# Retention attention with expert routing on one core: the second batch's heads swapped in q and k, state products and tails on quadrants of the array

## The chip, the cores and the metric

The kernel runs on one core of a Trainium2 chip. The metric is device time in microseconds of one execution. Three runs of the kernel before took 655.72, 658.25 and 662.20 us; the median is 658.25.

## What is computed

A retention layer (causal attention without softmax, its scores weighted by powers of a factor of each head) over 8 batches, 8 heads, 576 positions and 64 dimensions, and behind it a routed layer of 8 experts, each with a capacity of 576 of the 4608 tokens.

```python
scores = scale * np.matmul(q, k.transpose(0, 1, 3, 2))
gamma = 1.0 - 2.0 ** (-5.0 - np.arange(H, dtype=np.float32))
rel = pos[:, None] - pos[None, :]
Dmat = np.where(rel >= 0, gamma[:, None, None] ** rel[None, :, :], 0.0)
ret = scores * Dmat[None, :, :, :]
x = np.matmul(ret, v)                       # [tokens, heads * dims] afterwards
logits = x @ w_gate                         # each token goes to one expert with room, best logit first
h = np.maximum(x[mask] @ w1[e], 0.0)
out[mask] = h @ w2[e]
```

## The kernel before

The attention part works on 16 units. A unit `u` is one pair of batches and one pair of heads (`hp = u % 4`); four units make one pair of batches, `bp`. A unit has nine blocks of 128 columns: block `2*c + b` holds positions `128*c` to `128*c + 127` of batch `b` (`c` from 0 to 3), and block 8, the tail, the last 64 positions of both batches. Both heads of the pair stand on the partitions: head `h` of q and k on partitions `64*h` to `64*h + 63`.

The retention is computed in chunks of 128 positions. Each block gets scores within the block and, from a running state of the earlier chunks, what reaches across:

- `A` (L576): scores, k times q, 64 rows by 128 columns of the array. Head 0 uses rows 0 to 63, head 1 rows 64 to 127, and each writes its own PSUM tile `pA`. Four blocks fill the two tiles; the tail has its own (`pA0t`, `pA1t`). VectorE multiplies each by a mask with the powers of gamma of that head (L581, `am`).
- `ST` (L593): state products, v times scaled k, 128 rows by 64 columns, summed in PSUM over the chunks. Two ScalarE copies (L599), one for each head, scale the state into the two diagonal blocks of a 128x128 tile `S` whose other blocks are zero.
- `XS` (L620, L617 for the tail): state times q, 128 rows by 64 columns, because the zero blocks keep the heads apart. It writes the PSUM tile `pX`, three blocks to a tile, two tiles at a time.
- `XW` (L630): v times `am`, added into the same tile. `scale` (L642) then takes three blocks at a time out of PSUM into `xT`, times a factor for each position.
- `kscale2` (L556): GpSimd scales k into a new tile `ks`, a half unit ahead.

All these are fp32; each matmul of the program stands as two rows in the trace. The main loop runs over 16 units in two halves: blocks 0 to 3 and blocks 4 to 8. The scores are a half ahead: in the first half of a unit `A` does blocks 4 to 8 of that unit, in the second blocks 0 to 3 of the next. So a unit begins where the scores of its second half begin. In a half come, in this order: loads, the tail's XS of the unit before (first half), A, XS, ST, XW, ST, and then the side work that a table `fill` puts at this place. The order within each engine is that of the program.

The side work is for the pair of batches that was finished before: logits (L659 matmuls, L665, L672 transposes, L674), transposes of x on VectorE that are written to DRAM through SP's queue (L683, L688), and counts for the routing: `count_first` (L202 to L223) finds each token's best logit and its expert for three chunks of tokens at a time, `count_first_pe` (L234, L236) adds them up on TensorE.

Loads of q, k, v and of k by positions (`n`) of unit `u + 2` are put into SP's queue in unit `u`; q, k and v have three buffers each, `n` two. Constants (`cst`) have, for each pair of heads, two masks for the blocks, three factors and two masks for the tail, 896 columns in all. They are loaded between the first units.

## Time and profile before

| what | us |
|---|---|
| median of three runs (lowest, highest) | 658.25 (655.72, 662.20) |
| profiled execution | 662.15 |
| its span, first to last instruction | 660.4 |
| mean granted TensorE clock | 0.987 of full speed |
| TensorE matmuls busy | 622.7 (94% of the span) |
| VectorE busy | 420.4 (64%) |
| ScalarE busy | 272.6 (41%) |
| GpSimd busy | 174.9 (26%) |

The profile is of one execution. A row of a timeline gives the start of the first of some instructions that follow each other, how long they lasted together, the engine, the line of the kernel, the operation, the tile written and those read, and the shape; in brackets stand the idle time of the engine before it and what ended that. Matmuls overlap, and their ends are modelled; what counts is when the next one starts.

### The profile page before, as it was taken

To read this page: it belongs to the slowest core of one execution; us is meant where nothing else is said; L and a number is where in the kernel's file an instruction comes from. 1 tells how busy PE (TensorE), PEld (TensorE's weight loads), DVE (VectorE), ACT (ScalarE), POOL (GpSimd) and SP (SyncE) were. 2 spreads that over 40 slices of the span, in tenths; PEclk is the share of its full clock that TensorE was granted. 3 is DMA by queue.
4 is the path that set the end of the run, shared out by engine and by line. 5 is a ranking of instruction groups with operands and counts; after the bars stand their busy time and mean duration, and the time that the engine had idled before them with its cause. 6 is when DMAs were issued, how large, how long until landed. Compare 5 with 4: busy or idle time off the path is not lost.

```text
span 660.4 us, 14578 instructions
## 1 busy us (share of the span) xinstructions
PE 622.7 (94%) x5624; PEld 533.1 (81%) x5628; DVE 420.4 (64%) x1594; ACT 272.6 (41%) x488; POOL 174.9 (26%) x225
## 2 busy tenths in 40 slices
PE   7999898988888998999999999998999999999995
PEld 5887877776568876987998798788879989978984
DVE  3577979788775986887897798687774302311300
ACT  2333242423245344553455157225624734653501
POOL 2321222120031135134143142232224134231111
PEclk8999899999997999999999999999999999999998
DMA  9996999964369359689499568928865995893521
GB/s 335 402 403 176 317 295 283 351 195 129 129 193 224 71 190 251 165 235 241 130 235 225 165 163 204 256 82 204 198 196 128 217 261 149 187 254 122 97 64 40
DMA packets 51703, 134.75 MB, mean 204 GB/s; under 512 B 5810, under 2 KB 19762, under 8 KB 51634
## 3 DMA queue, kind: packets, MB, share of 16 engines
q1 hardware_dynamic: 36530, 81.65, 36.5%
q0 software_dynamic: 14960, 51.91, 35.8%
q8 instruction: 44, 0.72, 0.4%
q10 hardware_dynamic: 144, 0.26, 0.1%
q14 instruction: 25, 0.20, 0.1%
HBM read 81.90 MB, written 18.87 MB: 153 GB/s over the span
## 4 chain that ended last, share of the span: by engine, by line
PE 64%; DVE 14%; issue 9%; DMA 8%; ACT 2%; POOL 2%; SPq 1%; POOLq 0%; DVEq 0%; ACTq 0%
PE py L1021 23%; PE ph L982 22%; PE pX L630 4%; PE pA L576 3%; PE pX L620 3%; DMA cst<-in_cst 2%; PE pS L593 2%; PE r L335 2%; PE pt L953 2%; DVE xr L683 1%; DMA w1l<-raw 1%; PE pT L659 1%; DMA out_y<-yt,idx 1%; DMA kin<-in_qk 1%; DMA w2l<-raw 1%
## 5 line engine op out<-in xcount | busy, mean ns | idle before, releaser
L1021 PE MATMUL py<-w2h,hb 128*128 128x512 f32 x576 | 188.3, 399 | 0.0
L982 PE MATMUL ph<-xh,w1h 128*128 128x320 f32 (+1 forms) x512 | 153.3, 303 | 3.9 <-ACT xh L955 1.6
L982 PE MATMUL ph<-xh,w1l 128*128 128x320 f32 (+1 forms) x512 | 150.8, 298 | 3.2 <-DMA w1l<-raw 3.2
L982 PE MATMUL ph<-xl,w1h 128*128 128x320 f32 (+1 forms) x512 | 150.8, 298 | 0.5 <-issue 0.4
L1021 PE MATMUL py<-w2l,hb 128*128 128x512 f32 (+1 forms) x320 | 125.5, 392 | 0.3 <-DMA w2l<-raw 0.2
L1021 PEld LDWEIGHTS py<-w2h,hb 128*128 128x128 f32 x576 | 104.0, 188 | 20.8
L982 PEld LDWEIGHTS ph<-xh,w1h 128*128 128x128 f32 x512 | 97.4, 192 | 5.3 <-ACT xh L955 2.0
L982 PEld LDWEIGHTS ph<-xh,w1l 128*128 128x128 f32 x512 | 97.5, 192 | 3.4 <-DMA w1l<-raw 3.4
L982 PEld LDWEIGHTS ph<-xl,w1h 128*128 128x128 f32 x512 | 97.5, 192 | 1.8 <-issue 1.2
L986 ACT ACTIVATE hb<-ph 128x256 fp32r<-128x256 f32 (+1 forms) x128 | 51.5, 409 | 110.9 <-PE ph L982 102.3
L989 DVE SCALAR_TENSOR_TENSOR hb<-ph,hb 128x256 fp32r<-128x256 f32 (+1 forms) x192 | 58.7, 351 | 59.5 <-ACT hb L986 54.6
L599 ACT ACTIVATE S<-pS,cst 64x128 f32<-64x128 f32 x128 | 46.4, 362 | 91.4 <-PE pS L593 89.8
L998 POOL DMA_INDIRECT out_y<-yt,idx x40 | 41.1, 1026 | 119.5 <-ACT yt L1038 77.4
L1021 PEld LDWEIGHTS py<-w2l,hb 128*128 128x128 f32 (+1 forms) x320 | 56.7, 177 | 14.1 <-DMA w2l<-raw 1.5
L1038 ACT ACTIVATE yt<-py 128x512 f32<-128x512 f32 x32 | 19.1, 597 | 106.2 <-PE py L1021 79.5
L556 POOL TENSOR_TENSOR ks<-nin,cst 128x512 f32<-128x512 f32 x32 | 33.2, 1057 | 108.9 <-DMA nin<-in_vk 103.0
L926 POOL DMA_DIRECT2D w2l<-raw x32 | 28.8, 900 | 124.5 <-ACT hb L986 115.6
L937 POOL DMA_INDIRECT xg<-xd,idx x40 | 40.5, 1013 | 70.1 <-ACT w1h L921 36.8
L581 DVE TENSOR_TENSOR am<-pA,cst 128x512 f32<-128x512 f32 x64 | 41.0, 682 | 22.5 <-PE pA L576 16.0
L1041 DVE TENSOR_TENSOR yt<-yt,py 64x512 f32<-64x512 f32 x8 | 5.4, 678 | 70.2 <-ACT yt L1040 70.1
L926 POOL DMA_DIRECT2D w1l<-raw x31 | 27.5, 901 | 57.0 <-ACT w1l L925 47.0
L576 PE MATMUL pA<-qin,kin 64*128 64x128 f32 x512 | 39.1, 291 | 1.7 <-DMA qin<-in_qk 1.5
(186 smaller groups left out, 947.5 us busy)
## 6 DMA issues: line engine op xcount, KB each, us to landing
raw<-in_w SPq DMA_DIRECT2D x64, 512.0 KB, 5.9
w2l<-raw POOLq DMA_DIRECT2D x32, 512.0 KB
w1l<-raw POOLq DMA_DIRECT2D x31, 512.0 KB
kin<-in_qk SPq DMA_DIRECT2D x14, 576.0 KB, 7.8
qin<-in_qk SPq DMA_DIRECT2D x14, 576.0 KB
vin<-in_vk SPq DMA_DIRECT2D x14, 576.0 KB, 11.5
nin<-in_vk SPq DMA_DIRECT2D x14, 512.0 KB, 8.1
xd<-xr SPq DMA_DIRECT2D x36, 192.0 KB, 3.9
```

Of the source, the lines that this page charges most:

```text
L556: nc.gpsimd.tensor_tensor(KS[u][:, a:b], LD[u, 'n'].rearrange("p (a d) -> p a d", d=64)[:, a:b], ks[:, u % HP, a:b, None].to_broadcast([12 ...
L576: nc.tensor.matmul(PA[0][h][:, j], LD[u, 'k'][r, s], LD[u, 'q'][r, s], start=True, stop=True, skip_group_check=True)
L581: nc.vector.tensor_tensor(am, PA[0][h], m[:, None, h, :].to_broadcast([128, n, 128]), op=ALU.mult)
L599: nc.scalar.activation(st[64*h:64*h+64, :, 64*h:64*h+64], PS[u][64*h:64*h+64], AF.Copy, scale=ss[64*h:64*h+64, hp, c:c+1])
L630: nc.tensor.matmul(px[64*h:64*h+64, :], v[:, blk*128+64*h:blk*128+64*h+64], AM[g, h], start=False, stop=blk < 8, skip_group_check=True)
L926: nc.gpsimd.dma_start(lo, raw, accum_op=ALU.add)
L937: nc.gpsimd.indirect_dma_start(out=xg[:n, j, :], out_offset=None, in_=xd[:, :], in_offset=bass.IndirectOffsetOnAxis(ap=found[e][:n, j:j+1] ...
L982: T.matmul(ps, w, x, start=(k == 0), stop=(k == 11))
L986: A.activation(hb[:, f, c], ps, AF.Relu)
L989: V.scalar_tensor_tensor(hb[:, f, to+a:to+b], ps[:, a:b], 0.0, hb[:, f, 256*s+a:256*s+b].bitcast(F32), op0=ALU.max, op1=ALU.subtract)
L998: st = nc.gpsimd.indirect_dma_start(out=out[:, :], out_offset=bass.IndirectOffsetOnAxis(ap=found[e][:n, t:t+1], axis=0), in_=y[:n], in_off ...
L1021: T.matmul(ps[:m], a, w, start=(k == 0), stop=(k == last), skip_group_check=True)
```

## The change

q and k of the second batch of a unit have the two heads swapped on the partitions. So with `r` for the half of the rows, head `h` and batch `b`, `r = h ^ b`: the states of the two heads of both batches fill all four quadrants of a 128x128 tile, without zeros, and state times q is four matmuls of 64 rows by 64 columns that use the four quadrants. The powers of gamma move from the masks and from k into v, which GpSimd scales in place, and into a factor for each position; the masks hold ones and zeros and are the same for all heads. One VectorE instruction masks both heads, one ScalarE copy takes a state out. `pA` and `pX` are tiles of two banks each, one of each kind; `pX` holds four blocks of a half and, in the second half, the tail. The tail's products are quadrants too, and come at the end of their own unit behind the eviction of the second half. The counts take nine chunks of tokens at once, except for the last pair of batches. `n` gets a third buffer, and v is fetched ahead of it.

```diff
-    c = np.arange(4)
-    ks = g.reshape(HP, 1, 1, 2)[None] ** (-(128.0 * c[None, None, :, None, None] + p[:, None, None, None, None]))
...
+    vs = g.reshape(HP, 1, 2)[None] ** -at[:, None, :, None].astype(np.float64)
+    m1 = p[:, None] <= p[None, :]
+    m2 = p[:, None] % 64 <= np.arange(64)[None, :]
+    ex = 0.125 * g.reshape(HP, 2)[:, p // 64].T[:, :, None] ** np.arange(S)
...
+    cross = lambda a: np.where(second, a[:, :, ::-1], a)
...
     def count_first(s, c0, c1):
-        s.nc.vector.tensor_tensor(G, s.cand128[:, None, :].to_broadcast([128, 3, 128]),
-                                  s.m[:, c0:c1, None].to_broadcast([128, 3, 128]), op=ALU.is_le)
...
+        for c in range(c0, c1, 3):
+            G = s.pool.tile([128, 3, 128], BF16, name="G0", bufs=3)
...
-        part(80 + 896*hp + (0 if hp else 256), 976 + 896*hp)
+        part(CST + S*hp, CST + S*hp + S)
...
-    fetch("k0 q0 c n0 v0 k1 q1 h0 n1 v1 K0 Q0 h1 N0 V0 K1 Q1 N1 V1")
+    fetch("k0 q0 c v0 n0 k1 q1 h0 v1 n1 K0 Q0 h1 V0 N0 K1 Q1 V1 N1")
...
+    half = lambda x: slice(64*x, 64*x + 64)
+    FOUR = ((0, 0), (1, 0), (1, 1), (0, 1))
+    def vscale(u, a, b):
+        v = LD[u, 'v'][:, 128*a:128*b].rearrange("p (a d) -> p a d", d=64)
+        nc.gpsimd.tensor_tensor(v, v, vs[:, u % HP, 2*a:2*b, None].to_broadcast([128, 2*(b-a), 64]), op=ALU.mult)
...
+    def A(u, hf):
+        pa = two.tile([128, 2, 4, 128], F32, name="pA", tag="A", bufs=1)
...
+        nc.vector.tensor_tensor(AM[u, hf], pa, m1[:, None, None, :].to_broadcast([128, 2, 4, 128]), op=ALU.mult)
+    def A2(u):
...
+                nc.tensor.matmul(pa[half(r), h], k[half(r), s], q[half(r), s], start=True, stop=True, skip_group_check=True)
...
+    def ST(u, c):
...
+                nc.tensor.matmul(PS[u][half(h ^ b), b], n[:, s], v[:, s], start=(c == 0 and b == 0), stop=False, skip_group_check=True)
+        st = P['w'].tile([128, 2, 64], F32, name="S", bufs=4)
+        nc.scalar.activation(st, PS[u], AF.Copy)
...
+    def across(u, cs):
+        for c in cs:
+            for h, b in FOUR:
+                r = half(h ^ b)
+                o, a = (PX[u, c//2][half(h), b, 128*(c % 2):128*(c % 2)+128], 256*c + 128*b) if c < 4 else (PX[u, 1][half(h), b, 256:320], 1024 + 64*b)
+                nc.tensor.matmul(o, SI[u, c-1][r, b, :], q[r, a:a+o.shape[1]], start=c in (1, 2), stop=False, skip_group_check=True)
...
+    def within2(u):
+        for h, b in FOUR:
+            r = half(h ^ b)
+            nc.tensor.matmul(PX[u, 1][half(h), b, 256:320], LD[u, 'v'][r, 1024+64*h:1088+64*h], AM[u, 2][r, h],
+                             start=False, stop=False, skip_group_check=True)
+    def evict(u, c0, c1):
...
+        nc.vector.tensor_tensor(dst, src, e, op=ALU.mult)
...
     for u in range(16):
+        for hf in range(2):
...
+            A(u + hf, 1 - hf)
+            if hf == 0:
+                A2(u)
+            PX[u, hf] = two.tile([128, 2, 512], F32, name="pX", tag="X", bufs=1)
+            across(u, (2, 3) if hf else (1,))
+            ST(u, 1 + 2*hf)
+            within(u, hf)
+            if u == 15 and hf:
+                for c in (2, 3):
+                    evict(u, c, c + 1)
+            else:
+                evict(u, 2*hf, 2*hf + 2)
+            ST(u + hf, 2 - 2*hf)
+            if hf:
+                within2(u)
+                across(u, (4,))
+                evict(u, 4, 5)
+            fills(gs)
```

The new functions stand on these lines of the changed kernel: A L564 and L566, A2 L575 and L577, ST L587, across L599, within L608, within2 L615, evict L628.

On TensorE, at the end of a unit, before: the tail's L630 follows the other blocks, then the state products of the next unit, the tail's XS (which belongs to the next unit's first half) and the next scores.

```order
L630 MATMUL pX<-am0t,vin 64x128
L630 MATMUL pX<-am1t,vin 64x128
L593 MATMUL pS<-vin,ks 64x64 [waits DMAHW1_49,Activation_49,Pool_49]
L593 MATMUL pS<-vin,ks 64x64 x3
L617 MATMUL pX<-qin,S_120 64x64 x4
L576 MATMUL pA_1101<-qin,kin 128x128 [waits DVE_49]
L576 MATMUL pA_1102<-qin,kin 128x128 [waits DVE_49]
```

The same place after:

```order
L608 MATMUL pX<-am,vin 64x128 x8
L587 MATMUL pS<-vin,nin 64x64 [waits DMAHW5_49,DMAHW6_49,Activation_49,Pool_49]
L587 MATMUL pS<-vin,nin 64x64 x3
L615 MATMUL pX<-amt,vin 64x64 [waits DVE_49]
L615 MATMUL pX<-amt,vin 64x64 x3
L599 MATMUL pX<-qin,S 64x64 x4
L564 MATMUL pA<-qin,kin 128x128 [waits PE_49]
L564 MATMUL pA<-qin,kin 128x128 x7
```

The tail's L615 has moved behind the state products, and it waits for VectorE.

On VectorE, in the middle of a unit of the second pair of batches, with side work between two evictions, before (`xr` are the transposes, `mx` to `G` a count of three chunks, `om` to `FT` the routing's digits and tables):

```order
L683 STREAM_TRANSPOSE xr<-xT 128x4x4x32
L223 TENSOR_TENSOR G_1013<-rc_f,m 128x384 [waits DVE_49]
L214 TENSOR_TENSOR oh<-t_498,mx_499 128x24 [waits DVE_49]
L156 TENSOR_SCALAR om<-m 128x9
L158 TENSOR_TENSOR om<-m,om 128x9 [waits DVE_49]
L177 TENSOR_TENSOR dg<-om,sm 128x5x9 [waits DVE_49]
L177 TENSOR_TENSOR dg<-dg,sm 128x5x9 [waits DVE_49]
L179 TENSOR_TENSOR DF<-dg,inc 128x5x9 [waits DVE_49]
L181 TENSOR_TENSOR D_512<-dg,inc 128x3x18
L193 TENSOR_TENSOR FT_519<-kt,DF 128x512 [waits DVE_49]
L642 TENSOR_TENSOR xT<-pX,cst 128x384 [waits PE_49]
L581 TENSOR_TENSOR am_1111<-pA_1101,cst 128x512 [waits PE_49]
```

After, in the second half of such a unit, the count of nine chunks between two evictions:

```order
L197 TENSOR_REDUCE m<-Lg 128x9 [waits DVE_49]
L199 TENSOR_TENSOR t_473<-Lg,m 128x72 [waits DVE_49]
L201 TENSOR_TENSOR t_473<-t_473,decb 128x72 [waits DVE_49]
L205 TENSOR_SCALAR m<-m 128x9
L207 TENSOR_REDUCE mx_474<-t_473 128x9 [waits DVE_49]
L665 STREAM_TRANSPOSE xr<-xT 128x4x4x32
L219 TENSOR_TENSOR G_941<-rc_f,m 128x384 [waits DVE_49]
L209 TENSOR_TENSOR oh<-t_473,mx_474 128x72 [waits DVE_49]
L219 TENSOR_TENSOR G_944<-rc_f,m 128x384
L566 TENSOR_TENSOR am<-pA,cst 128x1024 [waits PE_49]
L628 TENSOR_TENSOR xT<-pX,cst 128x2x2x128 [waits PE_49]
L628 TENSOR_TENSOR xT<-pX,cst 128x128 [waits PE_49]
```

The seven small instructions of a count stand once, for 9 and 72 columns instead of 3 and 24, and two evictions follow the am.

## Rows read from the trace of the kernel before

**Rows 1.** The table by stages, each row a stretch of the span in us, its length, and then the busy time (and instructions) of TensorE's matmuls, its weight loads, VectorE, ScalarE and GpSimd; last the granted clock, the DMA share and GB/s. The second and the third are attention, without and with side work; the fourth ends it.

```profile
9.00:42.00 33.00, 31.82 (x549) 28.59 (x546) 20.27 (x65) 11.62 (x34) 9.39 (x10) 0.96 1.03 404
42.00:146.00 104.00, 98.44 (x1632) 82.56 (x1630) 85.61 (x228) 36.64 (x98) 22.95 (x22) 0.98 0.87 282
146.00:158.00 12.00, 9.59 (x145) 6.20 (x141) 9.92 (x35) 3.15 (x8) 0.00 (x0) 1.00 0.43 100
```

**Rows 2.** The timeline of unit 3, from the scores of its second half at 34.10 to those of unit 4 at 41.67: TensorE's matmuls, and of ScalarE and VectorE what the text uses. Behind it the row at which unit 15 begins, and the group of all state copies (count, busy us, mean ns).

```profile
34.10 1.16 PE L576 MATMUL pA<-qin,kin 64*128 64x128 f32 x16
...
35.09 0.27 PE L576 MATMUL pA0t<-qin,kin 64*128 64x128 f32 x1
...
35.21 0.27 PE L576 MATMUL pA0t<-qin,kin 64*128 64x128 f32 x1
...
35.41 0.66 PE L620 MATMUL pX<-qin,S 128*64 128x128 f32 x8
...
35.90 0.40 PE L593 MATMUL pS<-vin,ks 128*64 128x64 f32 x8
36.13 1.05 PE L630 MATMUL pX<-am,vin 128*64 128x128 f32 x16
36.41 0.75 ACT L599 ACTIVATE S<-pS,cst 64x128 f32<-64x128 f32 x2 [1.63 <-PE pS L593]
...
37.30 0.45 PE L593 MATMUL pS<-vin,ks 128*64 128x64 f32 x8
...
37.69 1.16 PE L576 MATMUL pA<-qin,kin 64*128 64x128 f32 x16
...
38.78 1.09 PE L620 MATMUL pX<-qin,S 128*64 128x128 f32 x16
38.88 1.29 DVE L581 TENSOR_TENSOR am<-pA,cst 128x512 f32<-128x512 f32 x2 [0.57 <-PE pA L576]
...
39.70 0.40 PE L593 MATMUL pS<-vin,ks 128*64 128x64 f32 x8
39.93 1.05 PE L630 MATMUL pX<-am,vin 128*64 128x128 f32 x16
...
40.59 0.56 DVE L642 TENSOR_TENSOR xT<-pX,cst 128x384 f32<-128x384 f32 x1 [0.42 <-PE pX L630]
...
41.06 0.45 PE L593 MATMUL pS<-vin,ks 128*64 128x64 f32 x8
...
41.31 0.43 PE L617 MATMUL pX<-qin,S 128*64 128x64 f32 x8
...
41.67 1.16 PE L576 MATMUL pA<-qin,kin 64*128 64x128 f32 x16
...
145.22 0.38 PE L576 MATMUL pA<-qin,kin 64*128 64x128 f32 x2
...
L599 ACT ACTIVATE S<-pS,cst 64x128 f32<-64x128 f32 x128 | 46.4, 362 | 91.4 <-PE pS L593 89.8
```

**Rows 3.** VectorE's groups by form between 42 and 146 us: line, operation, tiles, shape and count; behind the bar the busy us, the mean ns of one, and the idle time before them.

```profile
L581 DVE TENSOR_TENSOR am<-pA,cst 128x512 f32<-128x512 f32 x44 | 28.2, 680 | 6.7 <-PE pA L576 6.5
L642 DVE TENSOR_TENSOR xT<-pX,cst 128x384 f32<-128x384 f32 x33 | 18.1, 547 | 3.1 <-PE pX L630 2.9
...
L214 DVE TENSOR_TENSOR oh<-t,mx 128x24 bf16<-128x24 bf16 x9 | 3.2, 360 | 0.0
L581 DVE TENSOR_TENSOR am0t<-pA0t,cst 128x128 f32<-128x128 f32 x11 | 3.1, 278 | 0.0
...
L206 DVE TENSOR_TENSOR t<-t,decb 128x24 bf16<-128x24 bf16 x9 | 2.7, 297 | 0.0
L210 DVE TENSOR_SCALAR m<-m 128x3 f32<-128x3 f32 x9 | 2.3, 257 | 0.0
...
L204 DVE TENSOR_TENSOR t<-Lg,m 128x24 bf16<-128x24 f32 x9 | 1.8, 203 | 0.3
...
L212 DVE TENSOR_REDUCE mx<-t 128x3 bf16<-128x24 bf16 x9 | 1.6, 175 | 0.0
L202 DVE TENSOR_REDUCE m<-Lg 128x3 f32<-128x24 f32 x9 | 1.3, 144 | 0.0
L236 DVE TENSOR_TENSOR room<-room,cnt 128x8 f32<-128x8 f32 x8 | 1.2, 148 | 3.0 <-PE cnt L234 3.0
```

**Rows 4.** The timeline around the longest wait of XS, at 72.74, and the row of a table by stretches (as in rows 1) from 72 to 76 us.

```profile
70.14 0.51 DVE L223 TENSOR_TENSOR G<-rc_f,m 128x384 bf16<-128x384 f32 x1
...
72.14 0.55 DVE L642 TENSOR_TENSOR xT<-pX,cst 128x384 f32<-128x384 f32 x1
...
72.74 0.44 PE L620 MATMUL pX<-qin,S 128*64 128x128 f32 x4 [1.90 <-DVE xT L642]
...
72.00:76.00 4.00, 3.26 (x41) 3.12 (x43) 2.92 (x9) 0.92 (x3) 2.04 (x2) 0.64 0.95 210
```

**Rows 5.** The timeline where unit 2's data and constants arrive: its first scores, GpSimd's scaling, and VectorE and TensorE at 25.19.

```profile
21.36 1.16 PE L576 MATMUL pA<-qin,kin 64*128 64x128 f32 x16 [0.27 <-DMA qin<-in_qk]
...
24.10 2.04 POOL L556 TENSOR_TENSOR ks<-nin,cst 128x512 f32<-128x512 f32 x2 [6.17 <-DMA nin<-in_vk]
...
25.19 1.29 DVE L581 TENSOR_TENSOR am<-pA,cst 128x512 f32<-128x512 f32 x2 [4.25 <-DMA cst<-in_cst]
...
25.19 0.45 PE L593 MATMUL pS<-vin,ks 128*64 128x64 f32 x8 [0.32 <-POOL ks L556]
```

More of the change, by code (lines that the diff above doesn't have):

```diff
@@ L569, in A @@
                 nc.sync.dma_start(wg[:, :, 0:8], wg_d.rearrange("(hp p) e -> p hp e", p=128))
-        n, j, tail = (4, blk % 4, "") if blk < 8 else (1, 0, "t")
-        if j == 0: PA[0] = [P['ps'].tile([128, n, 128], F32, name=f"pA{h}" + tail, tag="y" if tail else "h0", bufs=2) for h in range(2)]
-        s = slice(blk*128, blk*128+128)
-        for h in range(2):
-            r = slice(64*h, 64*h+64)
-            nc.tensor.matmul(PA[0][h][:, j], LD[u, 'k'][r, s], LD[u, 'q'][r, s], start=True, stop=True, skip_group_check=True)
@@ L577, in A @@
-        if j == n - 1:
-            m = (m2 if tail else m1)[:, hp]
-            for h in range(2):
-                am = P['w'].tile([128, n, 128], F32, name=f"am{h}" + tail, bufs=2)
-                nc.vector.tensor_tensor(am, PA[0][h], m[:, None, h, :].to_broadcast([128, n, 128]), op=ALU.mult)
-                for i in range(n): AM[g-j+i, h] = am[:, i]
+        pa = two.tile([128, 2, 4, 128], F32, name="pA", tag="A", bufs=1)
+        for j in range(4):
+            s = slice(512*hf + 128*j, 512*hf + 128*j + 128)
+            for r in range(2):
+                nc.tensor.matmul(pa[:, r, j], LD[u, 'k'][half(r), s], LD[u, 'q'][half(r), s], start=True, stop=True, skip_group_check=True)
@@ L588, in ST @@
         v = LD[u, 'v']
-        for b in range(2):
-            blk = 2*c + b
+        for j in range(4):
+            c, b = divmod(j, 2)
             for h in range(2):
-                nc.tensor.matmul(PS[u][64*h:64*h+64, b], KS[u][:, blk*2+h, :], v[:, blk*128+64*h:blk*128+64*h+64],
-                                 start=(c == 0 and b == 0), stop=False, skip_group_check=True)
-        st = Sb[cnt[0] % NS]; cnt[0] += 1
-        for b in range(2):
-            SI[u, b, c] = st[:, b]
-        for h in range(2):
-            nc.scalar.activation(st[64*h:64*h+64, :, 64*h:64*h+64], PS[u][64*h:64*h+64], AF.Copy,
-                                 scale=ss[64*h:64*h+64, hp, c:c+1])
@@ L622, in XW @@
-    def XW(gs):
-        for g in gs:
-            u, blk, px = px_of(g)
-            if blk == 0 and u % HP == 0:
-                XT[u//HP] = P['xt'].tile([128, HP, 1152], F32, name="xT")
-            v = LD[u, 'v']
-            for h in range(2):
-                nc.tensor.matmul(px[64*h:64*h+64, :], v[:, blk*128+64*h:blk*128+64*h+64], AM[g, h],
-                                 start=False, stop=blk < 8, skip_group_check=True)
-            if blk in (2, 5) or g == 16*NB - 2:
-                scale(g)
@@ L738, in attention @@
             at(g1+4 if bp < NP-1 else g1+(1 if k == 0 else 2), logits2, bp, b0, b0+3)
-            it = R.count_first(c0, c0+3)
-            if bp < NP-1:
-                for i in range(6):
-                    at(g1+5+i, next, it, None)
-                at(g1+13, lambda c0: R.count_first_pe([c0], **tag()), c0)
-            else:
+            if bp == NP-1:
+                it = R.count_first(c0, c0+3)
                 if k == 0:
@@ L749, in attention @@
                     at(G-1, lambda it, k: rest(both(it, R.first_digits(27, 30) if k else iter(()))), it, k)
+            elif k == 2:
+                it = R.count_first(9*bp, 9*bp+9)
+                for i in range(8):
+                    at(g1+5+i//2, next, it, None)
+                at(g1+13, lambda bp: R.count_first_pe([9*bp, 9*bp+3, 9*bp+6], bank), bp)
         if bp < NP-1:
@@ L758, in attention @@
             at(g0+24+2*n, R.first_table, i, 2*bp+a, 2*bp+b)
-    kscale(0)
-    kscale2(0, 0, 8)
+    vscale(0, 0, 4)
     P['warm'](7)
-    for g in range(4):
-        A(g)
+    A(0, 0)
     ST(0, 0)
-    kscale2(0, 8, 16)
+    vscale(0, 4, 9)
     nc.gpsimd.memset(wg, 0.0)
@@ L1102, in build, with open_banks, bank @@
         P['warm'] = warm
+        banks = ExitStack()
+        def open_banks(name):
+            P['pb'] = banks.enter_context(tc.tile_pool(name=name, bufs=1, space=bass.MemoryType.PSUM))
+            return P['pb']
+        def bank(tag, shape, name, dt=F32):
+            return P['pb' if tag[0] == "h" else 'ps'].tile(shape, dt, name=name, tag=tag, bufs=1 if tag in "tr" else 2)
+        P['open'], P['close'], P['bank'] = open_banks, banks.close, bank
+        top.callback(banks.close)
         with ExitStack() as ctx:
```

186 lines of the change are left out of this document (69 added, 117 removed).

## The prediction

> **What bounds the kernel now.** I read the stage table first, then one plain unit of the attention stage on the timeline, then VectorE's groups, then the places where TensorE stops. A unit is one pair of heads with one pair of batches; there are 16.
>
> The stages [rows 1]: the attention part runs to about 158 us, and everything that the change edits lies in it. From 9 to 42 us TensorE counts as busy for 31.8 of 33 us, VectorE for 20.3, and the DMA share is 1.03 at 404 GB/s. From 42 to 146 us TensorE has 98.4 and VectorE 85.6 of 104 us, the DMA 0.87. A busy TensorE row does not say that its time is well spent: ends are modelled and steps overlap, so I go by starts.
>
> One unit without side work is on the timeline from 34.10 to 41.67 us [rows 2]: 7.57 us, 3.59 in the first half and 3.98 in the second. The reader is to see the beat. Two matmuls of different tiles start together, and the next two 0.11 us later (pA0t at 35.09 and 35.21) where they have 128 columns; eight state products of 64 columns take 0.23 (35.90 to 36.13), or 0.059 a step. Changing the form of the array costs extra: 16 score matmuls are 8 steps, 0.89, but take 0.99 to the next (34.10 to 35.09); pA0t to XS is 0.20 where a step is 0.11; XS then takes 0.49 for 4 steps; state products that start at 37.30 and need 0.23 are followed by scores at 37.69, 0.16 later. So about 0.15 a change, and there are four in a unit. One wait stands in it: the state products at 37.30 could have come after 8 steps of L630, at 37.02, but ScalarE's two copies end at 36.41 + 0.75 = 37.16; they come 0.28 late.
>
> With side work the units are longer: from 41.67 to 145.22, 11 units in 103.55 us, 9.41 each [rows 2] (units 4 to 14). There VectorE is the second bound: its queue is in order, and L620 at 72.74 stood 1.90 us for an xT that lay behind counting work [rows 4].
>
> **The change part by part.** All sums are against the profiled execution, 662.15 us with a span of 660.4; that is 3.9 us above the median of the runs shown, 658.25. I take the same gain off both.
>
> TensorE, per unit, in steps. *State times q:* blocks 2 to 7 are 12 matmuls in pairs, two passes each, 12 steps of 0.11 = 1.33; as quadrants four start together if they overlap four at a time: 6 steps, 0.67, so -0.67. The tail of it, 4 steps of 0.059, becomes 2: -0.12. The tail's L630, 2 steps of 0.11, becomes 2 of 0.059: -0.10. The tail's scores use two quadrants only (rows r to partitions r), 4 steps of 0.059 for 2 of 0.11: nothing. No row shows a quadrant matmul. Bounds: four at a time as above, or two at a time, which gives +0.9 on these three terms against the first reading. I take four, by the rows that are nearest: both row pairs (L576) and column pairs (L620) overlap fully at 0.11.
>
> The Trainium skill has a rule against it (TensorEngine Tiling (Array Packing), Gotcha 1: PSUM Pressure): different row tiles cannot access one PSUM bank at the same time. Before, the two row tiles write pA of two banks; after, rows 0 and rows 1 write one bank of pX, on different partitions. No run here shows such a pair. If that made them take turns, the sum would be that of two at a time, the second rival.
>
> *Changes of form:* four become seven (scores to quadrants, quadrants to state products, state products to scores; in the second half the same, and state products to the tail's quadrants). Three more at 0.15: +0.45. A change into quadrants is in no row; bounds 0 and 0.19, the two parts of one into scores.
>
> *State copies:* two ACTIVATEs of 64 partitions (362 ns each [rows 2], the pair 0.75) become one of 128 partitions with as many columns, about 0.37. The 0.28 goes: -0.28. What is late next at that place is the eight steps of L630 themselves.
>
> *A new wait:* the tail's matmuls (within2) write the bank that evict reads, and wait for it. From the last step of L630, VectorE starts after 0.22 (its modelled 0.27 less a step of 0.11 that is counted already, and 0.06: xT at 40.59 follows the fourth step of L630, whose end is 39.93 + 3 x 0.11 + 0.27 = 40.53), takes 0.68 for 512 columns (L581's 680 ns [rows 3]), and TensorE goes on 0.05 later as at 72.74: 0.95. State products cover 0.25 of it: +0.70, in which one change of form is hidden: +0.55. Behind the waiting matmul stand the tail, the logits and transposes of the side work and the next unit's scores; VectorE itself waits for the tail before its last evict, some 0.5 us with nothing to do.
>
> Sum per unit: -0.67 - 0.12 - 0.10 - 0.28 + 0.45 + 0.55 = -0.17: 7.4 us for a plain unit.
>
> VectorE, per unit. Two am of 512 columns, 1.29 a pair, become one of 1024. By 680 ns at 512 and 278 at 128 [rows 3] a column costs 1.05 ns, so 1.22: -0.14 for two. The two tail masks become one: -0.2. Three evicts at 547 become 680 + 680 + 278: +0.0. Counting once for nine chunks saves two of three runs of seven small instructions in each four units: 144 + 203 + 297 + 257 + 175 + 360 + 148 ns [rows 3] = 1.58, twice, less 0.2 for longer rows: -3.0, or -0.74 a unit. Together -1.1, against 0.5 of new idleness: -0.6 where VectorE is the bound.
>
> GpSimd scales v (18 blocks of 64) instead of k (16): 2.11 becomes 2.4 us a unit. It is busy 23.0 of 104 us [rows 1] and v now lands before n, so nothing; without that cover the first state products of a unit would come 0.3 us late. Buffers of n go from 2 to 3, SP's order is the same otherwise; the DMA share of 0.87 leaves it room.
>
> *The start:* constants shrink. Before unit 2's scores 1872 columns have come, now 1416: 456 x 512 B at 404 GB/s = 0.58 us off the wait at 21.36 [rows 5]. There, VectorE's am of unit 2 waited for its own masks until 25.19, the state products for ks until 25.19; with one mask for all heads and v ahead of n both go, about 1.0. With two plain units at -0.17: -1.9 by 41.67, where unit 4 begins.
>
> From 41.67 to 145.22: between -0.17 (TensorE bounds) and -0.6 (VectorE bounds) a unit. But both PSUM tiles are now single, so a half with much VectorE side work stops TensorE at the evict. I take -0.33, 11 times: -3.6. After that nothing: u = 15 does its logits later, but without the waits that stood among them. The first two terms are -5.5: 656.6 profiled, 652.7 on the median.
>
> **The rivals.** *VectorE bounds all of the middle, and its new idleness is filled* by an early PSUM release or by work that was late anyway: 11 x 1.1 + 1.9 = -14, 644. For it: 85.6 of 104 us with lumps in which it never rests. Against: TensorE counts as busy for 98.4 of the same 104 us, and its plain unit loses only 0.17.
>
> *Quadrants go two at a time:* +0.9 a unit turns -0.17 into +0.7; 11 units with VectorE taking a part of it 4 to 7, and at the start 2, less 1.9: +6, 664. For it: the skill's rule above; against: every pair of tiles in the rows overlaps fully.
>
> *The evict behind the side work, slower:* pX was three tiles in two banks, with a bank to go on with; now both banks are one half's. After evict of the first half VectorE does its side work, then am, then the evict for which the tail waits. TensorE comes there 3.4 us after the first half's last step, VectorE 0.9 + side work + 1.22 after it: it decides from 1.2 us of side work in a half. Counting nine chunks at once puts about 3 us into one half and 2.3 into the next: 1.8 + 0.7 and 0.5 for the rest, 3 us in four units, 8 in all; and stops of 2 us have cost clock (72 to 76 us ran at 0.64 of full speed, 1.4 us [rows 4]): three of those, 4. With -0.17 a unit and -1.9: +8, 666. Against: the same lump cost 1.90 at 72.74 before.
>
> **How the numbers follow.** The forecast has 0.48, its own range 648 to 657 (VectorE's -0.6 throughout, or no gain in the middle); the first rival 0.20, the second 0.15, the third 0.12; 0.05 is for what I do not see. Faster by over 1%, about what a measurement of this kernel can tell from none, means below 651.7: the first rival and 0.4 of the forecast, 0.41 with a share of the rest. Slower means above 664.8: most of the third and 0.4 of the second, 0.19. Same: 0.40. The range runs from the first rival to just under the third, 644 to 665.
>
> **What would show it.** Right: four starts of L599's kind within 0.03 us and 0.11 to the next four; a plain unit of 7.3 to 7.5 us; within2 some 0.7 us after the state products before it; no wait for the state copies; unit 4 beginning near 39.8 instead of 41.67. Wrong: quadrant steps in pairs (second rival), waits over 1.5 us for xT in the halves with counting and a clock of half speed behind them (third), VectorE without idle time between its last two evicts (first), or a first matmul stage after the attention that is not earlier by what the attention gained.

## The result and the profile after

The changed kernel takes 663.19 us (median of 20 runs, 657.11 to 667.40) where the kernel before takes 659.78 on the same chip: 1.0055 of it, 95% interval 1.0032 to 1.0078. On two other chips the ratio was 1.0058 and 1.0057. It is some 3.6 us slower; 5.5 us faster was forecast. Ratios here and below are estimated from the single runs, without the few that were over 1.5% slower than the fastest of their kernel, and so differ a little from the quotient of two medians. The span of its profiled execution is 662.8 us (before 660.4).

The stages, against [rows 1]; the end of the attention is some 4 us later:

```profile
9.00:42.00 33.00, 28.88 (x578) 25.13 (x578) 20.41 (x50) 4.45 (x16) 10.71 (x10) 0.95 1.03 401
42.00:150.00 108.00, 91.87 (x1707) 74.54 (x1709) 83.44 (x153) 16.65 (x53) 26.02 (x22) 0.95 0.82 269
150.00:162.00 12.00, 9.61 (x153) 6.63 (x153) 9.18 (x30) 1.82 (x5) 0.00 (x0) 0.88 0.35 84
```

A plain unit of the changed kernel, against the timeline of [rows 2] (`ST` is L587, `across` L599, `within` L608, `within2` L615, `evict` L628):

```profile
26.11 1.16 PE L564 MATMUL pA<-qin,kin 64*128 64x128 f32 x16
...
29.29 1.16 PE L564 MATMUL pA<-qin,kin 64*128 64x128 f32 x16
...
30.38 0.67 PE L599 MATMUL pX<-qin,S 64*64 64x128 f32 x16
...
30.98 0.45 PE L587 MATMUL pS<-vin,nin 128*64 128x64 f32 x8
...
32.14 0.40 PE L587 MATMUL pS<-vin,nin 128*64 128x64 f32 x8
32.35 0.69 DVE L628 TENSOR_TENSOR xT<-pX,cst 128x512 f32<-128x512 f32 x1 [0.63 <-PE pX L608]
...
33.10 0.34 PE L615 MATMUL pX<-amt,vin 64*64 64x64 f32 x8 [0.56 <-DVE xT L628]
...
33.49 0.38 PE L564 MATMUL pA<-qin,kin 64*128 64x128 f32 x2
```

It lasts from 26.11 to 33.49: 7.38 us, forecast 7.4. The 16 rows of L599 take 0.60 to the next line, change of form included; eight pairs at 0.11 would need 0.88, so four quadrants run at once (four start within 0.02 us, the next four 0.11 later). The tail's products wait for the eviction.

Now TensorE where unit 4 begins (41.52, 41.91), and where the units that hold the count of nine chunks (6, 10 and 14) begin and end; first after, then the starts of before that answer:

```profile
41.52 0.34 PE L615 MATMUL pX<-amt,vin 64*64 64x64 f32 x8 [1.60 <-DVE xT L628]
...
41.91 0.38 PE L564 MATMUL pA<-qin,kin 64*128 64x128 f32 x2
...
59.98 0.38 PE L564 MATMUL pA<-qin,kin 64*128 64x128 f32 x2
...
70.45 0.34 PE L615 MATMUL pX<-amt,vin 64*64 64x64 f32 x8 [3.57 <-DVE xT L628]
...
70.84 0.53 PE L564 MATMUL pA<-qin,kin 64*128 64x128 f32 x2
...
98.57 0.38 PE L564 MATMUL pA<-qin,kin 64*128 64x128 f32 x2
...
110.04 0.58 PE L564 MATMUL pA<-qin,kin 64*128 64x128 f32 x2
...
138.38 0.38 PE L564 MATMUL pA<-qin,kin 64*128 64x128 f32 x2
...
149.33 0.51 PE L564 MATMUL pA<-qin,kin 64*128 64x128 f32 x2
```

```profile
60.83 0.38 PE L576 MATMUL pA<-qin,kin 64*128 64x128 f32 x2
...
68.94 0.37 PE L576 MATMUL pA<-qin,kin 64*128 64x128 f32 x1
...
99.28 0.38 PE L576 MATMUL pA<-qin,kin 64*128 64x128 f32 x2
...
107.39 0.39 PE L576 MATMUL pA<-qin,kin 64*128 64x128 f32 x2
...
136.42 0.38 PE L576 MATMUL pA<-qin,kin 64*128 64x128 f32 x2
```

Units 4 to 14 took 103.55 us before [rows 2] and take 149.33 - 41.91 = 107.42 now. Units 6, 10 and 14 went from 8.11, 8.11 and 8.80 us to 10.86, 11.47 and 10.95: +8.26. The other eight together gained 4.39, 0.55 each on average (unit 7 gained 1.51, unit 11 lost 0.25). The waits of L615 add up to 19.9 us: 3.57, 3.94 and 3.65 in units 6, 10 and 14, 1.60 in unit 3, and 0.56 to 0.86 in each of the others, with side work or without. Before, L620's waits for xT added up to 5.4. Two more profiles of the changed kernel (e5, e13) have 106.64 and 106.98 us for units 4 to 14; of the kernel before there is one.

What VectorE does in unit 6 while TensorE stands, with GpSimd's row:

```profile
63.04 0.69 DVE L628 TENSOR_TENSOR xT<-pX,cst 128x512 f32<-128x512 f32 x1 [0.43 <-PE pX L608]
...
64.42 2.26 POOL L546 TENSOR_TENSOR vin<-vin,cst 128x512 f32<-128x512 f32 x2 [13.44 <-DMA vin<-in_vk]
...
64.76 0.80 DVE L199 TENSOR_TENSOR t<-Lg,m 128x72 bf16<-128x72 f32 x1
...
65.59 1.15 DVE L201 TENSOR_TENSOR t<-t,decb 128x72 bf16<-128x72 bf16 x1
...
66.66 0.16 DVE L205 TENSOR_SCALAR m<-m 128x9 f32<-128x9 f32 x1
...
68.58 1.22 DVE L566 TENSOR_TENSOR am<-pA,cst 128x1024 f32<-128x1024 f32 x1
69.72 0.68 DVE L628 TENSOR_TENSOR xT<-pX,cst 128x512 f32<-128x512 f32 x1
```

From 63.74 to 68.58, 4.84 us, side work stands between the first half's eviction and the next mask. Two instructions take 0.80 and 1.15 us while GpSimd scales v; L205 takes 0.16 once it has stopped.

Behind the attention: the first weights are fetched at 179.96 (175.38 before), the first product of layer two starts at 230.01 (223.89), the last rows go out at 657.1 (654.7). From that first product to the last rows it is 426 to 433 us in all the twenty profiles of this study, whose instructions are the same there; no run explains that spread.

### The profile page after: what moved, and what is told of

The parts are those of the page before. It is cut to its first block, busy times and chain, and to the rows that moved or that the text cites. A ratio compares the mean times of both kernels' runs of the same rounds, so it can differ in the third digit from the quotient of the medians.

```text
span 662.8 us, 14684 instructions
## 1 busy us (share of the span) xinstructions
PE 613.2 (93%) x5756; PEld 522.0 (79%) x5756; DVE 418.0 (63%) x1504; ACT 244.8 (37%) x424; POOL 179.0 (27%) x221
## 4 chain that ended last, share of the span: by engine, by line
PE 66%; DVE 17%; DMA 8%; issue 5%; ACT 2%; POOL 2%; SPq 0%; POOLq 0%; DVEq 0%; ACTq 0%
PE ph L960 24%; PE py L999 24%; PE pA L564 4%; PE pX L608 3%; DVE xT L628 2%; DMA qin<-in_qk 2%; PE pX L599 2%; DMA raw<-in_w 2%; PE pS L587 2%; PE pt L931 2%; PE r L332 1%; DMA w1l<-raw 1%; PE pT L641 1%; DMA w2l<-raw 1%; DVE am L566 1%
## 5 line engine op out<-in xcount | busy, mean ns | idle before, releaser
L546 POOL TENSOR_TENSOR vin<-vin,cst 128x512 f32<-128x512 f32 (+1 forms) x32 | 37.6, 1194 | 106.3 <-DMA vin<-in_vk 88.2
L589 ACT ACTIVATE S<-pS 128x128 f32<-128x128 f32 x64 | 17.8, 278 | 119.4 <-PE pS L587 119.4
L566 DVE TENSOR_TENSOR am<-pA,cst 128x1024 f32<-128x1024 f32 x32 | 39.0, 1220 | 21.6 <-PE pA L564 21.6
L564 PEld LDWEIGHTS pA<-qin,kin 64*128 64x128 f32 x512 | 34.3, 204 | 11.8 <-issue 2.7
L564 PE MATMUL pA<-qin,kin 64*128 64x128 f32 x512 | 40.8, 303 | 3.0 <-DMA qin<-in_qk 2.6
```

Source lines behind the costliest of these rows:

```text
L546: nc.gpsimd.tensor_tensor(v, v, vs[:, u % HP, 2*a:2*b, None].to_broadcast([128, 2*(b-a), 64]), op=ALU.mult)
L564: nc.tensor.matmul(pa[:, r, j], LD[u, 'k'][half(r), s], LD[u, 'q'][half(r), s], start=True, stop=True, skip_group_check=True)
L566: nc.vector.tensor_tensor(AM[u, hf], pa, m1[:, None, None, :].to_broadcast([128, 2, 4, 128]), op=ALU.mult)
```

## The experiments

The theories, as the texts on record name them. A: the concentrated count stands ahead of the eviction that the tail waits for. B: the single pX and the tail behind the eviction cost the same whatever the side work is. C: in the texts of e2 and e3, VectorE bounds the units and the waits only move; in those of e6 and e17, GpSimd's scaling stretches VectorE's small instructions, and so C is used below. D: counting nine chunks at once costs by itself. K: the half clock behind long stops is a cost of its own. T and V: TensorE, or VectorE, bounds the units with side work. Ratios are to the kernel before on the same chip, with 95% intervals; runs of one group share a chip.

| group | run | median us | ratio |
|---|---|---|---|
| 1 | e1_count3 | 664.31 | 1.0034 (1.0001 to 1.0067) |
| 1 | e2_tail_first | 661.33 | 0.9972 (0.9941 to 1.0003) |
| 1 | e3_both | 653.97 | 0.9873 (0.9836 to 0.9910) |
| 1 | e4_before_count9 | 673.21 | 1.0159 (1.0111 to 1.0208) |
| 2 | e5_after_again | 663.53 | 1.0058 (1.0035 to 1.0082) |
| 2 | e6_noscale | 659.87 | 1.0015 (0.9993 to 1.0036) |
| 2 | e7_count9_spread | 662.89 | 1.0051 (1.0029 to 1.0073) |
| 2 | e8_spread_tail | 655.18 | 0.9933 (0.9903 to 0.9962) |
| 3 | e9_fill | 664.63 | 1.0013 (0.9985 to 1.0040) |
| 3 | e10_twice | 673.67 | 1.0139 (1.0095 to 1.0183) |
| 3 | e11_both_again | 653.98 | 0.9831 (0.9784 to 0.9879) |
| 3 | e12_both_fill | 652.66 | 0.9828 (0.9783 to 0.9873) |
| 4 | e13_after | 667.48 | 1.0057 (1.0028 to 1.0086) |
| 4 | e14_count3 | 664.07 | 1.0004 (0.9968 to 1.0039) |
| 4 | e15_both | 652.82 | 0.9804 (0.9755 to 0.9854) |
| 4 | e16_both_twice | 668.46 | 1.0069 (1.0036 to 1.0101) |
| 5 | e17_both_act | 651.68 | 0.9880 (0.9849 to 0.9912) |
| 5 | e18_both_base | 650.25 | 0.9885 (0.9835 to 0.9936) |

Lengths of units in one profile of each, us from start to start as above. Before and in e1, e10, e15 and e16, the counts of three stand in units 4 to 6, and the same again in 8 to 10 and 12 to 14; after and in e4, the count of nine stands in unit 6, and TensorE's part of it in unit 7. From profile to profile of one kernel, units 4, 5 and 8 repeat to 0.1 us; unit 7 does not (8.66 in e1, 12.92 in e14).

| run | 4 | 5 | 6 | 7 | 8 | units 4 to 14 |
|---|---|---|---|---|---|---|
| before | 10.07 | 9.09 | 8.11 | 11.17 | 10.09 | 103.55 |
| e4 (before, count of nine) | 10.07 | 8.93 | 9.55 | 13.27 | 10.09 | 112.60 |
| after | 9.43 | 8.64 | 10.86 | 9.66 | 9.42 | 107.42 |
| e1 (counts of three) | 9.42 | 8.81 | 8.10 | 8.66 | 9.42 | 101.14 |
| e10 (e1, q's products twice) | 10.20 | 9.57 | 8.99 | 13.75 | 10.19 | 114.00 |
| e15 (counts of three, tail ahead) | 8.94 | 8.33 | 7.55 | 8.40 | 9.01 | 92.75 |
| e16 (e15, q's products twice) | 9.71 | 9.09 | 8.21 | 12.15 | 9.71 | 106.37 |

**The count and the place of the tail.** e1 and e14 give the changed kernel the counts of three chunks, spread as before; e2 puts the tail's products ahead of the eviction; e3, e11, e15 and e18 do both; e4 gives the kernel before the count of nine; e5 and e13 are the changed kernel.

```diff
+                for i in range(6):
+                    at(g1+5+i, next, it, None)
+                at(g1+13, lambda c0: R.count_first_pe([c0], bank), c0)
...
-            elif k == 2:
-                it = R.count_first(9*bp, 9*bp+9)
-                for i in range(8):
-                    at(g1+5+i//2, next, it, None)
-                at(g1+13, lambda bp: R.count_first_pe([9*bp, 9*bp+3, 9*bp+6], bank), bp)
```

```diff
             within(u, hf)
+            if hf:
+                within2(u)
+                across(u, (4,))
...
+            if hf:
+                evict(u, 4, 5)
             ST(u + hf, 2 - 2*hf)
-            if hf:
-                within2(u)
-                across(u, (4,))
-                evict(u, 4, 5)
```

> The changed kernel with the counts of the kernel before: three chunks at a time, spread over the side work. Theory A: the changed kernel loses in three places (once for each of the first three pairs of batches) where the count of nine chunks stands on VectorE ahead of the eviction that the tail waits for: 3 stops of TensorE of 3.6 to 3.9 us instead of 0.65, and half clock behind each. Then without the nine the waits of L615 for xT fall from 19.9 us to 11 to 13, the two additional stretches of half clock go, and the time is 10 to 13 us under the changed kernel's, less 2 for more instructions on VectorE: 651 to 655, below the kernel before. Theory B: the single pX and the tail behind the eviction cost this whatever the side work is (the lump only moves): at most 3 us under the changed kernel, 660 to 663.

> The changed kernel with the tail's products ahead of the eviction of the second half and ahead of the next unit's state products, so that the tail waits for nothing; both evictions stand together. Theory A: the 0.65 us wait of a plain unit goes 16 times (10 us), and of the three long stops the part that the next scores can cover (1.3 us each, 4 us), if VectorE's idle time between its last two evictions goes as well: 648 to 652. Theory C, VectorE bounds the units and the waits only move to the next state products times q: 658 to 662, with L599 waiting for xT in place of L615.

> Both edits: counts of three chunks and the tail ahead of the eviction. Theory A: the gains add but for the part of the long stops that both take: 641 to 647, no wait of TensorE for xT over 1.5 us and one stretch of half clock in the attention part. Theories B and C: not below 655.

> The kernel before with only the counts of nine chunks. Theory A: it saves VectorE 2 us for each pair of batches but puts 4 to 5 us of it ahead of one eviction; with pX in two tiles TensorE stops 1.5 us less than in the changed kernel, so three stops of about 2 and a stretch of half clock more: 658 to 664, within 1% of the kernel before. Theory D, the fewer instructions help wherever pX has two tiles: 650 to 655.

> The changed kernel as it is, beside the three that follow. Its own trace had 19.9 us of waits for xT in front of the tail's last products, with three stops of 3.6 to 3.9 us. The same is expected here, and 0.3 to 0.8 per cent above the kernel before of this chip.

> The changed kernel, beside the next two on one chip: 1.003 to 1.008 of before.

> The same with the counts of three chunks. If the count of nine chunks costs on top of the wait for the eviction (it cost 1.6 per cent alone on the kernel before): 0.989 to 0.997 of before, at least 0.6 per cent under the changed kernel. If the two are the same lost time: 0.999 to 1.006, within 0.4 per cent of it, and only the next run is faster.

> Counts of three chunks, the tail's products ahead of the eviction: 0.982 to 0.989 of before, as in two runs on other chips. By the theory that the wait for the eviction is the first loss, 1.2 per cent or more under the run before this.

Group 4 has the chain on one chip: 1.0057, then 1.0004 without the count of nine, then 0.9804 with the tail ahead. By the medians the count costs 3.4 us on top of the wait for the eviction, and the wait 11.3 us; the spread of the runs leaves each open to 2 or 3 us. Alone on the kernel before the count costs 10.5 us, and where the tail is ahead (e2 against e3) 7.4: with the tail behind, the two are partly the same lost time. So it is from the other side: with the count of nine in place, the tail's move is worth 0.8% (e2 against the changed kernel on other chips), some 5.5 us. In units without a long stop the tail's move saves 0.48 us (units 4 and 5 of e1 and e15), 7.7 over 16 units; that the rest of the 11.3 lies in the stops is a reading and not shown apart. The waits of e14 and of e15 from 9 to 158 us (engine, line and what it waited for; us, times, longest):

```profile
PE pX L615 <- DVE xT L628: 12.6, 16, 1.9
PE pA L564 <- DVE am L566: 6.2, 3, 2.9
```

```profile
PE pA L564 <- DVE am L566: 2.4, 2, 1.2
...
PE pX L599 <- DVE xT L628: 1.9, 1, 1.9
```

The reader is to see that L615 no longer waits in e15.

Several totals were missed. e1 came out 9 us above theory A's 651 to 655, and just above B's 660 to 663, though its waits of L615 (11.4 us) and its one stretch of half clock are as A said. e2 lies in the 658 to 662 of its theory C: its long waits moved, but to L564 for am (9.7 us in four waits) and not to L599. e3 (653.97) is slower than A's 641 to 647 and faster than what B and C allowed. e4 is slower than either theory said, with waits of up to 1.8 us for am and 3.5 for xT. e14 is in the range of its second theory, though 0.5% under e13 and not within 0.4; e11 and e15 lie a little under their ranges, e18 a little over. B is out: e15 has the single pX and is 2% faster than before.

**The count spread.** e7 keeps nine chunks and puts two steps into each of four halves; TensorE's part of the count (L231) comes right behind the last of them. e8 adds the tail ahead.

```diff
-                for i in range(8):
-                    at(g1+5+i//2, next, it, None)
-                at(g1+13, lambda bp: R.count_first_pe([9*bp, 9*bp+3, 9*bp+6], bank), bp)
+                for i, b in enumerate((5, 5, 8, 8, 13, 13, 17, 17)):
+                    at(g1+b, next, it, None)
+                at(g1+19, lambda bp: R.count_first_pe([9*bp, 9*bp+3, 9*bp+6], bank), bp)
```

> The changed kernel, the count of nine chunks kept, its steps put two to a half over four halves instead of six in one half. Theory A (too much side work in one half ahead of the eviction): the side work of the half falls from 4.84 us to 2.1-2.6, the waits for xT from 19.9 us to 11-13, no stop above 2 us, unit 15 begins at 140 to 143 us instead of 149, and the time is 3 to 6 us below the changed kernel. Theory D (that nine chunks are counted at once costs by itself): the stops stay and the time within 1.5 us of the changed kernel.

> Both: the count of nine chunks spread over four halves, and the tail's products ahead of the eviction. With counts of three chunks the second edit gave 0.987 of the kernel before and a plain unit of 6.9 us. Theory A: about the same here, 0.983 to 0.989, since VectorE has some 90 instructions less than with three chunks, at about 0.1 us each at most 3 us apart and mostly beside other work. Theory D: above 0.993.

The long stops go in e7 (none over 2.2 us) and the time stays. Unit 6 takes 8.18 us instead of 10.86, but unit 7, which now has the rest of the count, 11.23 instead of 9.66, and unit 8 11.80 instead of 9.42. Three stretches of 6.8 us at 1.2 GHz fall behind the waits of units 7, 11 and 15; the first:

```profile
76.00:84.00 8.00, 7.22 (x97) 5.97 (x97) 4.89 (x11) 0.55 (x2) 2.26 (x2) 0.57 0.83 267
```

```profile
77.88 2.08 PE L564 MATMUL pA<-qin,kin 64*128 64x128 f32 x16
...
81.42 1.86 PE L608 MATMUL pX<-am,vin 128*64 128x128 f32 x16
```

There VectorE is busy for 4.89 of 8 us, TensorE for 7.22 at a granted clock of 0.57, and 16 scores take 2.08 us where 1.16 is their time at full clock. So the 2.4 us that unit 8 lost are read as the half clock's; no run fills these waits.

e8 is faster than before, but by less than theory A expected (0.983 to 0.989), and less than with three chunks. Its 0.9933 lies on theory D's side (above 0.993), but its trace shows another cause: L231 stands right behind the last steps of the count and waits for them, and half clock follows (the waits of e8 from 9 to 158 us, in total, times, longest):

```profile
PE cnt L231 <- DVE G L219: 5.6, 2, 3.0
```

In e15 no such wait stands in these units. So the place of L231 is part of what e8 lacks; whether nine chunks cost by themselves, these two runs do not decide.

**The half clock.** e9 fills the three stops of the changed kernel, e12 a stop behind the attention.

```diff
             if hf:
+                if u in (6, 10, 14):
+                    P['warm'](14)
                 within2(u)
```

> The changed kernel; in the second halves of units 6, 10 and 14, where TensorE stops for 3.6 to 3.9 us in front of the tail's last products, 14 products of constants (0.21 us each at full clock, 3.0 us, written to a tile that nobody reads) are put into the stop. The wait for VectorE stays. Theory K (the half clock behind these stops is a cost of its own): the stretches of half speed at 71, 108 and 149 us (3.4, 6.8 and 3.4 us) vanish, unit 15 begins 3 to 5 us earlier than at 149.3, and the time falls by 3 to 5 us. Rival: behind a stop VectorE is what is late, and the half clock costs nothing: less than 1 us.

> The same, with 15 products of constants (3.2 us at full clock) in the first expert's stop of 3.55 us for the w1l tile, behind which TensorE ran 3.4 us at half speed without a gap. Theory K: that stretch vanishes and 1.2 to 1.8 us are gained, 0.2 to 0.3 per cent. Rival (the weights' transfers bound that stage, DMA share 1.0): nothing, or the stretch only moves to the next stop.

The window of unit 6 in the changed kernel, then in e9 (columns as in [rows 1]):

```profile
62.00:76.50 14.50, 10.60 (x189) 9.15 (x186) 13.27 (x29) 1.67 (x6) 4.92 (x4) 0.88 0.74 261
```

```profile
62.00:76.00 14.00, 11.55 (x190) 8.52 (x186) 12.81 (x27) 1.39 (x5) 4.56 (x4) 1.00 0.79 268
```

The clock stays at 2.4 GHz in e9, and from the tail's mask of unit 6 to that of unit 7 it is 13.94 us against 13.79; for units 10 and 14 13.45 and 12.81 against 13.61 and 12.60. Units 4 to 14 take 107.40 us in e9 and 107.42 in the changed kernel. VectorE is busy for 13.27 of 14.5 us and is what is late: the half clock costs nothing there. The time of e9 lies 0.4% lower than the changed kernel's on other chips, with intervals that just touch; its trace does not show where. In e12 the half clock after the attention is gone, and from the first product of layer one to the first of layer two it is 34.2 us where e11 has 38.8; but in the other profiles, which fill nothing there, this stretch takes from 34.0 to 39.0 us, and the two times differ by less than their intervals. So e12 shows no gain.

**The quadrants.** e10 (three chunks) and e16 (tail ahead too) issue every state product with q twice, which changes x: what the quadrants took away is put back.

```diff
-        for c in cs:
+        for c, again in [(c, x) for c in cs for x in (0, 1)]:
```

> The changed kernel with the counts of three chunks, and every product of state and q issued twice (added twice into the same place), 6 steps of 0.11 us and 0.12 us for the tail more in each unit, 0.78 us, 12 us in the whole program if TensorE bounds every unit: what the quadrants took away is put back. Theory T (TensorE bounds, in the middle too): 9 to 13 us above the same kernel without the doubling (1.0034 of before on another chip), so 1.017 to 1.024 of before. Theory V, the prediction's (VectorE bounds the units with side work, which get half or less of what TensorE gains): 3 to 7 us, 1.008 to 1.014 of before.

> The changed kernel with the counts of three chunks and the tail's products ahead of the eviction, which gave 0.987 of before on another chip, again as the base of the next: 0.984 to 0.991 of before.

> That kernel with every product of state and q issued twice (added twice into the same place): 0.78 us of TensorE more in each unit, 12 us in all. If TensorE bounds every unit there: 10 to 14 us above the run before this one, 1.5 to 2.1 per cent, so the quadrants are worth what the steps take. If VectorE bounds the units with side work: 3 to 7 us, 0.5 to 1.1 per cent.

e16 is 15.6 us over e15 for 12.5 us of steps, and e10 1.05% over e1 and 1.35% over e14, 7 to 9 us, between what V and T expected (on other chips). The lengths of units tell more. Units 4, 5 and 8 hold side work, and the doubling makes each of them 0.76 to 0.78 us longer in e10 and 0.70 to 0.77 in e16: all of the steps. TensorE bounds these units, as T says, with the tail behind the eviction too, and the quadrants are worth there what they save. In units 7 and 11 of e16 stand two waits for am of 2.9 and 2.7 us, as e14 has them by chance (see GpSimd), so its 15.6 us are not the steps alone. Why e10's total rose by less than 12.5 us is not shown.

**GpSimd.** e6 leaves out the scaling of v in units 7, 11 and 15; e17 gives it to ScalarE.

```diff
-            if blk == 2:
+            if blk == 2 and u + 1 not in (7, 11, 15):
                 vscale(u + 1, 0, 4)
-            if blk == 5:
+            if blk == 5 and u + 1 not in (7, 11, 15):
                 vscale(u + 1, 4, 9)
```

```diff
+        for j in range(2*a, 2*b):
+            v = LD[u, 'v'][:, 64*j:64*j+64]
+            nc.scalar.activation(v, v, AF.Copy, scale=vs[:, u % HP, j:j+1])
```

> The changed kernel, v of units 7, 11 and 15 not scaled by GpSimd (left out of the computation), since that scaling runs in the half that holds the count of nine chunks. Theory C (GpSimd at work stretches VectorE's small instructions): L199 and L201 go from 0.80 and 1.15 us to about 0.25 and 0.30, the side work of that half from 4.84 us to 3.4, the three stops from 3.6-3.9 us to 2.2-2.5, and the time 4 to 7 us below the changed kernel, the half-clock stretches with it. Theory A alone (the number of instructions in that half): the stops stay at 3.5 us or more and the time within 1.5 us of the changed kernel.

> Counts of three chunks, the tail's products ahead of the eviction, and v scaled by ScalarE: 18 activations of 64 columns in each unit from unit 1 on, 8 of them behind the third state product of the unit before, 10 behind its own second one, in place of two GpSimd instructions. Theory C (GpSimd at work stretches VectorE's small instructions in SBUF): none of VectorE's side instructions below 0.6 us gets longer than that in the attention, the waits of L564 for am fall below 1.5 us in all, and 2 to 6 us are gained on the run beside it. Rival: the 18 activations (some 0.2 us each, 3.6 us in a unit) stand ahead of ScalarE's state copies, which come late: a new wait of the products of L599 for S, no gain or up to 6 us lost.

> The base of the run before on the same chip: 0.980 to 0.988 of before.

In e6 the two instructions that took 0.80 and 1.15 us in unit 6 are short:

```profile
64.12 0.23 DVE L199 TENSOR_TENSOR t<-Lg,m 128x72 bf16<-128x72 f32 x1
64.39 0.20 DVE L201 TENSOR_TENSOR t<-t,decb 128x72 bf16<-128x72 bf16 x1
```

The longest wait of L615 is 2.1 us instead of 3.9, and the time is 3.7 us below e5: C holds, just under the 4 to 7 us that it expected. Units 6, 10 and 14 take 9.36, 9.38 and 9.36 us, 3.08 over before and not 8.26 (unit 7 takes 0.56 more). So more than half of what these units lost is GpSimd's stretching, and the rest the count's place. Two executions of one kernel (counts of three) show the same by chance, e14 first, then e1:

```profile
71.48 2.26 POOL L546 TENSOR_TENSOR vin<-vin,cst 128x512 f32<-128x512 f32 x2 [4.82 <-DMA vin<-in_vk]
71.53 1.07 DVE L176 TENSOR_TENSOR D<-dg,inc 128x54 bf16<-128x54 int32 x1
...
72.52 1.50 DVE L188 TENSOR_TENSOR FT<-kt,DF 128x512 bf16<-128x512 bf16 x1
...
75.21 0.58 PE L564 MATMUL pA<-qin,kin 64*128 64x128 f32 x2 [2.86 <-DVE am L566]
```

```profile
70.37 0.21 DVE L176 TENSOR_TENSOR D<-dg,inc 128x54 bf16<-128x54 int32 x1
70.50 0.42 DVE L188 TENSOR_TENSOR FT<-kt,DF 128x512 bf16<-128x512 bf16 x1
70.53 2.51 POOL L546 TENSOR_TENSOR vin<-vin,cst 128x512 f32<-128x512 f32 x2 [3.81 <-DMA vin<-in_vk]
70.84 1.22 DVE L566 TENSOR_TENSOR am<-pA,cst 128x1024 f32<-128x1024 f32 x1
```

In e14 v landed just ahead of the two instructions, in e1 just behind their start. That cost e14 a stop of 2.86 us (0.93 in e1), and its attention ended 6 us later than e1's. So one profile of this kernel tells the length of the attention only to some 6 us, and the chain of group 4 rests on times, not on profiles.

e17 has no such stretching: L188 has a mean of 420 ns (684 in e18), the waits for am are 0.9 us (5.9), and the attention keeps its full clock. It gains nothing. ScalarE, then the state products that wait for it, then the same state products in e18:

```profile
53.62 2.48 ACT L551 ACTIVATE vin<-vin,cst 128x64 f32<-128x64 f32 x10
...
54.10 0.95 PE L592 MATMUL pS<-vin,nin 128*64 128x64 f32 x8
```

```profile
52.19 0.40 PE L587 MATMUL pS<-vin,nin 128*64 128x64 f32 x8
```

Each of these products starts as one of ScalarE's instructions on v ends. That is 0.55 us more, some 8 us over the units as an estimate: the rival's loss, at another place than it said.

## Why the prediction was wrong

The step that failed is the middle, "I take -0.33, 11 times: -3.6": it measured +3.9.

- *It averaged over units that have different limits.* Units 4, 8 and 12 gained some 0.65 each, but not by VectorE's -0.6. They take 10.07 to 10.09 us on the kernel before with the counts in them or moved out (e4), 9.42 or 9.43 after with the count moved out or put back (e1), and doubled products lengthen them by all of the steps (e10): TensorE bounds them after the change, and less counting there is worth nothing. (A plain unit gained 0.19; where the other 0.46 comes from was not measured.) The merged count puts its work into units 6, 10 and 14, where VectorE is then late (13.27 of 14.5 us): +2.75, +3.36 and +2.15.
- *The third rival described this and got 0.12.* It priced the lump at 8 in all, and 8.26 was measured, in part by luck: it had no term for GpSimd's scaling beside the merged count, which is more than half of it (e6). Against it stood that "the same lump cost 1.90 at 72.74 before". It was not the same lump: with the count of nine the kernel before, spare bank and all, loses 10.5 us (e4).
- *The new wait.* As forecast in a plain unit: L615 starts 0.96 us behind the start of state products that need 0.23 (32.14 to 33.10), 0.73 for +0.70, and in ordinary units with side work it idles for the same 0.56 us. What the forecast left to its -0.33, "a half with much VectorE side work stops TensorE at the evict", were four long stops, in units 3, 6, 10 and 14: 12.8 of the 19.9 us. Putting the tail ahead of the eviction was worth 0.48 in a unit without such a stop, near the 0.55 of the sum, and 11.3 us in all with counts of three.
- *VectorE's saving.* The durations of the small instructions [rows 3] (297 ns for L206, 257 for L210) hold GpSimd's interference. Without it, in e17, the answering lines take 159 and 161 ns: seven add up to about 1.15 us, not 1.58, and merging saves some 0.5 a unit, not 0.74. And merged instructions met GpSimd again (L201: 1.10 us mean).
- *The start.* -1.9 was forecast; unit 4 begins at 41.91 and not at 39.8, 0.24 later than before. Two things were wrong. The scores of unit 2 still wait for q, and start 0.55 later than the 21.36 of before where 0.58 earlier was forecast (21.15 and 21.36 in e5 and e13):

```profile
21.91 1.16 PE L564 MATMUL pA<-qin,kin 64*128 64x128 f32 x16 [0.84 <-DMA qin<-in_qk]
```

  And in unit 3 VectorE casts tables while GpSimd scales v; after, then e15, where v landed later:

```profile
36.94 2.48 POOL L546 TENSOR_TENSOR vin<-vin,cst 128x512 f32<-128x512 f32 x2 [5.00 <-DMA vin<-in_vk]
...
37.16 2.57 DVE L140 CAST ct<-rc_f 128x576 bf16<-128x576 f32 x2
```

```profile
35.67 0.81 DVE L140 CAST ct<-rc_f 128x576 bf16<-128x576 f32 x2
```

  The casts take 1.76 us more, and TensorE waits 1.60 us at 41.52 instead of a plain unit's 0.56. Scaling on GpSimd was costed at nothing for being in time; its neighbour on VectorE was not looked at.
- *The clock.* The third rival charged 4 us for half clock behind the stops. The stretches came (71, 108 and 149 us), and filling the stops gained nothing in the attention (e9).
- *Right:* quadrants four at a time, the plain unit, no wait for state copies (one copy of 0.28 us), am of 1024 columns in 1220 ns and 686 for an eviction. The second rival, and with it the rule of the Trainium skill on row tiles and one PSUM bank (TensorEngine Tiling (Array Packing), Gotcha 1: PSUM Pressure), does not hold here: pairs would have taken 0.88 us where 0.60 was measured.

What stays open: with three chunks and the tail behind, the ratio is 1.0034 and 1.0004, where -0.17 us a unit and the start would have given 0.994. In e1's profile units 4 to 14 take 2.4 us less than before, in e14's 3.8 more. GpSimd's interference, as in e14, is one cause; how much of the rest is its doing was not measured. Nor was what the order of the loads and the third buffer of n are worth by themselves.

## What to carry to other kernels

Price side work in the half where it runs, ahead of the instruction that somebody waits for, and not as a mean: merging small instructions saved time where nobody waited and lost it by putting the sum where TensorE did. Look at what another engine does to SBUF in that half, too: here over half of what the three units lost came from GpSimd's scaling beside it. When double buffers are given up for a wider tile, put every product that shares the tile ahead of its eviction. Before charging a low clock, ask which engine is late there.
